# HGRN scan and Hyena gate on one core: a second order table, searched with late loads

## The chip, the cores and the metric

The kernel runs on one core of one Trainium2 chip. The metric is the device time of one execution in microseconds (us), the median over several runs of the same program. A core has TensorE (PE) for matmuls, VectorE (DVE), ScalarE (ACT) and GpSimd (POOL) for the rest, and SyncE (SP), which here only issues the DMAs. Each engine runs its own instructions in order and waits for the others on semaphores.

## The reference, cut to what matters

x and f_logit are 4 x 6272 x 256 in float32. First comes a gated recurrence along the sequence, then a gate with a long convolution (as long as the sequence, circular) between two matrix products:

```python
sig = 1 / (1 + np.exp(-f_logit))
f = lower_bound + (1 - lower_bound) * sig
for t in range(S):                       # S = 6272
    h = f[:, t] * h + (1 - f[:, t]) * x[:, t]
    y[:, t] = h
proj = y @ w_proj                        # 256 -> 3 * 256: x1, x2, x3
X2 = np.fft.rfft(x2, n=S, axis=1)
H = np.fft.rfft(filter_fft, n=S, axis=0)[None]
x2_conv = np.fft.irfft(X2 * H, n=S, axis=1)
out = (x1 * x2_conv * x3) @ w_out
```

## The kernel before, in words

**The stages.** The four batches are worked through one after the other, overlapped at their ends. `hgrn(b)` reads the sequence in 13 chunks (0 to 12) of 512 rows, the last of 128. For each chunk two loads of 512 KB bring f_logit (`FL`) and x (`XT`) into a slot (L318, the DMA is recorded at L331). ScalarE makes the sigmoid in place (`sig`, L334), GpSimd the product with x (`u`, L336). TensorE transposes both halves of the features (`su`, kh = 0 and 1, L348); ScalarE or VectorE turns the gate into f (`f`, L361 or L363), VectorE scans (`scan`, L369), and GpSimd copies the sequence's head behind its end (`wrap`, L292). The result h stays in SBUF (`HA`).

The convolution is a two-stage Fourier transform (6272 = 128 x 49) made of matmuls. `spectrum(b)` runs phase P (x2, L703, copied at L280 or L285), F1 (L716) into the region `A`, F2 (L778), the product with the filter's spectrum (on VectorE straight from PSUM, L801, or a copy on ScalarE and the product on GpSimd, L810), and I2 (L820). The filter's own spectrum is computed at the start and put out to DRAM (L660); `H` loads (L756) bring it back in parts for each batch. `gate(b)` makes x1 * x3 (L397, copies L282 and L287, product L418, or L427 on GpSimd). `phase_o(b)` goes over 13 groups (0 to 12): I1 (L883), the product `y` on VectorE into one of two buffers `ys` (L889), `proj` with w_out (L901), a copy `o` (L282 or L287) into one of six places (two buffers `osb`, two slots of `PP`, two halves of `A`), and the `store` (L913).

**Slots.** x and f_logit have three slots (`NX`), in the first batch three more. The loads of a chunk can be issued when the second transpose step (kh = 1) of the chunk three places before has run. "Chunk 3.11" below is chunk 11 of batch 3 (batches count from 0).

**Who sets the order.** Nothing is scheduled when the kernel is built. Every piece of work is recorded as an op (`Plan.op`, L77) with the engines that may run it, what it reads and writes, and for transfers `dma`, `lag` and `margin`, which `emit` does not read. Then `emit` (L108) runs the ops in the order of the string `ORDER` (L125 to L189): three characters each give the op's number, the engine that runs it and the PSUM bank.

```python
for i, e, b in self.order():
    o = self.ops[i]
    assert e in o["cost"] and i not in seen and o["preds"] <= seen
...
    o["fn"](*args)
```

The table was found by a search outside this file. So the position of a DMA in the string is its place in SP's queue, and SP waits at a load until its slot is free, at a store until its copy is done. An op of one engine that stands behind another op of the same engine can't pass it.

Of the kernel before, what the change touches and what calls it, by code (L numbers as in the profile page):

```python
# [61 lines left out]
class Plan:  # L62
# [63 lines left out]
    "A3gA7gAzgA/gAAYAOYAVIA0YA4AAhQAcQABIACIAPIASYAQAAWIAjQAaQAbQAdQAfQAgQAeQA5QA1SAoUBAYAiUA2KA8ABHgBfgBPgAlUBBUArWAnWBD"  # L126
    "gBLgBXgBTgBbgBjgA9WAsSA6ABIYBJSBCMBEYAyAARAAYUAwVDqgDrgDngAkVD2gECgADgD3gDpgEOgDogEDgEPgEagAqVBQIA+OAXIBFQAmVBRWAuVB"
    "SGApVBGAAZEBKKBYIAUIBMYBNSATYBUYAxVBZWBgABOKBaOAtVBVQBWABcIAvUBhWBiOBdUBkYBeEBlQBmIBpUBqMBwQBxIBnWBoODsAD4ADtYEEAB3U"
    "BuQBvIBrYAEYByYBsWBtOB4EDuSBzQB+UB0AB5WD5YDyQB/EB6GCAUEQACBEDvKDwKB7YEFYCCYB8SDzID0ID6WB9CCDUCEED+QCJSCQUD/AEcAEmgD7"
    "OD8OERYEbgCKKCRMCOWEAIEngEygEGSCHUCIMCPGEHCEIKEoAEdYCLYCSYEKWCTQELGCMUCUACNEEMOESSCZQETKCXWE0AEWUCaICYGCeQCgWEUKE8gE"  # L130
    "zgAFgE9gFGgFQgCGgEpYEJYCbYEXMEYME+ACfAChGCcSCdCEeQEiWEjGEfIEgICnUCoECpSEqUEkOAIACqCCjQCwSCuWErECiYE1YAJYCkAEsMEuQFIA"
    "CvGCsUCxKE2SCzWEvIEwICtEC+UC0GE3KE4KE5QCrYAHYAKYCyYC/EE/YE6ADAWE7IDBGC3UFASC5WFSAC4EDDQC6GFDUDEAC8WC9GEhYFHgFbgF6gFJ"
    "YCVgFRgCmgC7YFTYDCYFagCFgFkgFlgB2gFugCWgDGgFvgAGgFcAFBKFCKFKSDJQJTWJUXFEMFFMFLKDKAJWHJVODOUDPEFmAFMKDHQFNWDIAJYUFOOF"
    "POJaEFUSDQQFVCDRADMUFWKFXWFdYDNEFwAFnYDLYEtYALYDSYAMYEVYElYFxYDXQFYOFZOFeSDYADTUFfCFhQDUEDZWFgKFiADaGFjIFoUFpEDeSDfC"
    "DgWDhGFrQFySDcWFqMJZUJdVFzKF0KF1SFsAMugB1gC2gF4gGlgG3gF/gDWgClgDFgMigMWgF5gC1gMXgD1YEBYExYJXYANYDxYD9YDbYF7YF8YDiYFt"
    "IF2KF3KDdGDjWJbsJeQJiRENAEZAJfFGHSGTUJkBJgoDkOGVQGJWGWIGICMwAGUEGKOGXSGFQGZUGYCGGIGaEMkAGBWGRSGDUGSCGLQGNSGCOMYAGEMG"
    "MIGOKGPUGQEJjWJnXJoQJluJpHJqoGbUDmgDlgHAgMjgDVgGugGdSGhWGcEGeKGfQGmUJsSGiGGgAGosGqsF9WJuCJtTHTgHJQJxSJvrF+GGjUJzCGvW"
    "GkMHKAG4SHLUG8CG6CGrYMZYGxuGzuGnYGwYGpYGsQG5YJyWJ2SJ3TG9YG0YG7YGyYGtAHMEG1QHBUG2AJ0uJ4KJ5rHFsHDsHPWHNQJ7TJ8SKAVHQGG+"
    "WKBUJ9DHOAJ+qHRQHUSKCNHSIG/GHYCMlYHWqKFVKGQKHFKIoKDsHVYHCYHGYHEYHHWHcgMvgGAgHlgHdSHfqHhqHIGHmQH3WHZYKEYHqAHXYHaUHgYH"
    "eYHrYHooHpYHiYHnYH4GHbEKKSKLRKMCKNBH5WHjUH7SH6OHvQHugIBgHkEH8CH9UH+EHsWHzoHxoICSHtGH/UIAMIEqIGCKPRMaWKRBJwYHwYH0YMxY"  # L140
    "JcYHyYKOYIFYILUMbGMeQIPEIHYIDYMcOMfAH1SKQVH2CMgIKStIKgINsITgIcgM6gIvgIlWImGIISIJCIdQIfAIUWIWGIYuIhAMmSMqUIQYIZYIVYIM"
    "YJmYIOYIXYI4gM7gNGgNHgJBgMrEMnKMsMMoKKUWKWGIRQKVXKZWISAKXvIaQIwUI0sIiYIgYIeYM8AM9YI1YMdYIbAKbGInSIpQKaXKeWKfVKcvIysI"
    "oCIqAIrSKjXKgGIsCKlPIjQKkUKhtIkAKmsItSI5WIuKNIAMyQM2UMzAI7uI9GM0INSgJKgKoSKpTKtWKuXNTgKqCKrrKnYIxYKJYJrYNJYJhYIzYM3E"
    "M4MM+QKvGKwHI2SM/ANCWI3CNAIJCUKySKzTNKQJGsNDGJEENegNEOK0CK1rNOUK3SNUANLAJ/YKsYK2YI+YI8YI6YKdYKxYKTYJHYJ6YKYYJFYNVYI/"
# [840 lines left out]
```

## Time and profile before

| | us |
|---|---|
| median of 3 runs | 455.66 (455.5 to 456.23) |
| the profiled execution's own time | 457.66 |
| its span, first to last instruction | 455.5 |
| TensorE busy | 436.8 |
| VectorE busy | 407.9 |
| ScalarE busy | 392.8 |
| GpSimd busy | 307.6 |
| DMA from HBM and to it | 86.12 and 31.98 MB, 259 GB/s over the span |

PE is TensorE's matmuls, PEld its weight loads, which overlap them. "SPq" is SP's queue of DMA issues. In timelines the first two columns are the start and the length of a stretch in us, and the bracket at the end is the idle time of the engine before it with what ended it. In a list of waits the numbers are the total, how often, and the longest. The granted clock of TensorE was 0.998 of full speed.

### The profile page before, as it was taken

How to read it: one execution, taken by the hardware profiler on the slowest of the kernel's cores; microseconds unless marked ns; L12 is line 12 of the kernel's file. 1: busy time of each engine (PE TensorE's matmuls, PEld its weight loads, DVE VectorE, ACT ScalarE, POOL GpSimd, SP SyncE). 2: the span in 40 equal slices, each digit the busy share in tenths (PEclk: the TensorE clock that was granted, in tenths of full speed). 3: DMA queues.
4: the chain of work that ended last, by engine and by line, in shares of the span. 5: the costliest groups of instructions: out<-in, count | busy, mean ns of one | idle time of the engine just before them, and what ended most of it. 6: DMA issues, size and time to landing. Idle time of an engine off the chain costs nothing.

```text
span 455.5 us, 14537 instructions
## 1 busy us (share of the span) xinstructions
PE 436.8 (96%) x6017; PEld 344.1 (76%) x6017; DVE 407.9 (90%) x456; ACT 392.8 (86%) x545; POOL 307.6 (68%) x287
## 2 busy tenths in 40 slices
PE   8999999999999999999999999999999899999994
PEld 6877778667767889767768988776769797776783
DVE  5889998899999986999999987999999859988973
ACT  5789998889999988999988978999999778998354
POOL 4588994289998642889986626999996505657300
PEclk9999999999999999999999999999999999999999
DMA  8999979767797977559956893589586822763167
GB/s 326 406 402 380 373 254 362 275 217 242 273 322 237 333 250 316 173 172 325 357 195 232 308 358 146 179 293 339 192 309 210 349 115 89 219 199 111 47 266 302
DMA packets 42562, 119.04 MB, mean 261 GB/s; under 512 B 4096, under 2 KB 5760, under 8 KB 42496
## 3 DMA queue, kind: packets, MB, share of 16 engines
q1 hardware_dynamic: 42496, 118.11, 72.7%
q8 instruction: 47, 0.77, 0.7%
q14 instruction: 19, 0.16, 0.1%
HBM read 86.12 MB, written 31.98 MB: 259 GB/s over the span
## 4 chain that ended last, share of the span: by engine, by line
PE 58%; DVE 14%; ACT 8%; issue 5%; DMA 5%; POOL 3%; SPq 0%; DVEq 0%; ACTq 0%; POOLq 0%
PE PS L397 14%; PE PS L820 8%; PE PS L703 7%; PE PS L901 7%; DVE HA L369 6%; PE PS L348 6%; PE PS L716 5%; PE PS L778 5%; DMA FL<-in_f_logit_dram 3%; PE PS L883 3%; DVE ys L889 3%; DMA XT<-in_x_dram 2%; DVE fTs L363 2%; PE PS L633 2%; DVE PP L801 2%
## 5 line engine op out<-in xcount | busy, mean ns | idle before, releaser
L336 POOL TENSOR_TENSOR XT<-XT,FL 128x1024 f32<-128x1024 f32 (+1 forms) x47 | 105.1, 2239 | 59.5 <-ACT FL L334 31.7
L369 DVE TENSOR_TENSOR_SCAN HA<-fTs,HA,PS 128x512 f16<-128x512 f32 (+1 forms) x96 | 112.8, 1204 | 3.0 <-ACT fTs L361 2.2
L397 PE MATMUL PS<-HA,W 128*128 128x490 f16 (+1 forms) x416 | 100.4, 367 | 0.3 <-ACT XS L282 0.2
L810 POOL TENSOR_TENSOR PP<-HA,Hu 98x1008 f16<-98x1008 f16 x43 | 90.2, 2106 | 4.3 <-ACT HA L280 2.0
L280 ACT CAST HA<-PS 128x1024 f16<-128x1024 f32 (+1 forms) x106 | 83.5, 821 | 4.9 <-PE PS L716 1.8
L889 DVE TENSOR_TENSOR ys<-PS,zt 128x1024 fp32r<-128x1024 f32 (+1 forms) x52 | 58.5, 1153 | 9.7 <-PE PS L883 5.4
L801 DVE TENSOR_TENSOR PP<-PS,Hu 98x1008 f16<-98x1008 f32 x53 | 62.2, 1199 | 1.5 <-PE PS L820 0.7
L901 PE MATMUL PS<-Wo,ys 128*128 128x256 f32 x392 | 57.8, 293 | 3.3 <-DVE ys L889 2.6
L361 ACT ACTIVATE fTs<-PS,nomc 128x512 f32<-128x512 f32 (+1 forms) x84 | 55.8, 673 | 4.7 <-PE PS L348 2.3
L397 PEld LDWEIGHTS <-W 128*128 128x128 f16 x416 | 35.2, 97 | 29.9 <-issue 3.3
L820 PEld LDWEIGHTS <-PP 98*128 98x128 f16 x1024 | 48.9, 98 | 11.3 <-issue 2.9
L418 DVE TENSOR_TENSOR zt<-PS,XS 128x490 f16<-128x490 f32 (+1 forms) x86 | 54.7, 653 | 2.3 <-DVE XS L287 0.5
L282 ACT ACTIVATE XS<-PS 128x490 f32<-128x490 f32 (+1 forms) x85 | 49.0, 584 | 8.7 <-DVE zt L418 5.1
L901 PEld LDWEIGHTS PS<-Wo,ys 128*128 128x128 f32 x392 | 49.5, 188 | 8.3 <-ACT PP L282 1.5
L280 ACT CAST Th<-PS 128x784 f16<-128x784 f32 x63 | 51.7, 823 | 4.0 <-PE PS L820 3.3
L820 PE MATMUL PS<-VA,PP 98*128 98x98 f16 x512 | 52.0, 207 | 0.8 <-POOL PP L783 0.3
L820 PE MATMUL PS<-VB,PP 98*128 98x98 f16 x512 | 51.8, 207 | 0.0
L334 ACT ACTIVATE FL<-FL 128x1024 f32<-128x1024 f32 (+1 forms) x47 | 47.4, 1012 | 3.0 <-DMA FL<-in_f_logit_dram 2.8
L703 PE MATMUL PS<-W,HA 128*128 128x256 f16 x392 | 43.8, 273 | 0.0
L703 PEld LDWEIGHTS <-HA 128*128 128x128 f16 x392 | 42.8, 142 | 0.7 <-ACT XS L282 0.3
L348 PE MATMUL PS<-iden,FL 64*128 64x64 f32 x704 | 40.3, 230 | 2.7 <-ACT osb L282 1.4
L348 PEld LDWEIGHTS PS<-iden,FL 64*128 64x128 f32 x704 | 30.2, 138 | 15.1 <-DVE HA L369 3.4
(112 smaller groups left out, 764.8 us busy)
## 6 DMA issues: line engine op xcount, KB each, us to landing
FL<-in_f_logit_dram SPq DMA_DIRECT2D x43, 512.0 KB, 5.9
XT<-in_x_dram SPq DMA_DIRECT2D x43, 512.0 KB, 6.7
Hu<-H SPq DMA_DIRECT2D x39, 512.0 KB, 4.4
out_dram<-osb SPq DMA_DIRECT2D x24, 512.0 KB, 4.6
out_dram<-PP SPq DMA_DIRECT2D x16, 512.0 KB, 5.2
Hl<-H SPq DMA_DIRECT2D x13, 512.0 KB, 4.5
out_dram<-HA SPq DMA_DIRECT2D x8, 512.0 KB, 6.1
X<-in_moe_filter_fft_dram SPq DMA_DIRECT2D x7, 512.0 KB, 6.2
```

Of the source, the lines that this page charges most:

```text
L280: nc.scalar.copy(dst, src)
L336: op("u", {"POOL": 0.1 + 0.553 * nb}, lambda e, xt=xt, ft=ft: nc.gpsimd.tensor_tensor(xt, xt, ft, op=AOP.mult), r=[("ft", k)], w=[("xt", k)])
L348: nc.tensor.transpose(bank(pb)[:, at[p] + j:at[p] + hn:nb], src[ps, j, cols], iden[ps, ps])
L361: nc.scalar.activation(fT, sT, AF.Identity, scale=by, bias=1.0)
L369: nc.vector.tensor_tensor_scan(h, fT, bank(pb)[:, 512 - hn:512 + hn], init, op0=AOP.mult, op1=AOP.add),
L397: nc.tensor.matmul(PS[:, p, 0:n], W13[:, kh, js], HA[:, HB[kh] + t0:HB[kh] + t0 + n], start=(kh == 0), stop=(kh == 1))
L703: nc.tensor.matmul(pp[:, r - r0, :], column(HB[kh], q_of(r)), W2[:, kh, :], start=(kh == 0), stop=(kh == 1))
L801: nc.vector.tensor_tensor(pr, px.unsqueeze(1).broadcast_to([TB, 2, UE, 63]), hh(), op=AOP.mult)
L810: nc.gpsimd.tensor_tensor(pr, spec[:, o, :, 1:64].unsqueeze(1).broadcast_to([TB, 2, UE, 63]), hh(), op=AOP.mult)
L820: nc.tensor.matmul(PS[:, ib + o, pr * TB:(pr + 1) * TB], PP[:TB, k, o, n, 2 * pr:2 * pr + 2, :], v[:TB], start=(n == 0), stop=(n == 1))
L889: nc.vector.tensor_tensor(late["ys"][:, yk, :, 0:rn * 128], PS[:, cb:cb + 2, 0:rn * 128], late["zt"][:].rearrange("p k r m -> p k (r m)") ...
L901: nc.tensor.matmul(po[:, i, :], late["ys"][:, yk, kh, i * 128:(i + 1) * 128], Wo[:, kh, :], start=(kh == 0), stop=(kh == 1))
```

## The change

Only the string `ORDER` differs. The new table comes from a search that counted the loads of x and of the logit as landing far later than all other transfers; the ops, their numbers, their sizes and their code are the same, and so are the matmuls. All lines of the string change, since every op's place is in it:

```diff
--- before.py
+++ after.py
@@ -123,69 +123,69 @@
 ORDER = (
-    "A3gA7gAzgA/gAAYAOYAVIA0YA4AAhQAcQABIACIAPIASYAQAAWIAjQAaQAbQAdQAfQAgQAeQA5QA1SAoUBAYAiUA2KA8ABHgBfgBPgAlUBBUArWAnWBD"
...
-    "YElfQlZglmWlnGldCloglgIlhUlpWluQlqOlrSlvIlwQlxIliElegljglsCltglyg"
+    "AzgA3gA/gA7gBHgBDgBXgAAYAOYABIA0AAyYA4AAhQAcQAjQAaQAbQAdQAfQAgQAeQACIA5QA1SA8YAPIASIBAIAoUBBUBCMAiWAlWAQAARABIYA9WAr"
...
+    "PglmQlYGlpWlgKldMlnAlZglogleglhSlqOluUlrQlvMlwUlxMliCljglsAltglyg"
 )
```

Decoded, the two tables differ as follows. On SP (ft is a load of f_logit, xt of x, s a store of the batch that is being put out):

```
batch 0 to 1
before: s0, ft1.11, s1, s3, xt1.11, xt1.12, ft1.12, s2, ft2.0, ft2.1, s6, s5, xt2.2, ft2.2, s4, s8, ...
after:  ft1.11, s1, xt1.11, ft1.12, s2, s0, xt1.12, s5, ft2.0, ft2.1, ft2.2, s3, xt2.0, s8, xt2.2, ...
batch 1 to 2, after: ft2.11, xt2.11, s1, s0, s2, ft2.12, xt2.12, s3, ft3.0, ft3.1, ft3.2, xt3.1, s7, s8, s5, ...
  (before, s5, s3, s6 and s4 come ahead of the loads of batch 3)
batch 2 to 3
before: xt3.10, ft3.10, s0, s1, ft3.11, xt3.11, s4, s2, ft3.12, xt3.12, s7, s6, s3, s5, s8, s9
after:  ft3.10, xt3.10, s1, ft3.11, xt3.11, s3, s0, ft3.12, xt3.12, s2, s9, s4, s8, s6, s5
```

At the start w_out is loaded 25 places earlier and the logit of chunk 0.7 comes behind that of 0.8; some stores and loads of the filter's spectrum change places. On PE the order of steps is nearly the same, with neighbours exchanged: `su` 3.8, kh = 1, now comes ahead of one `proj` and two `I1` of batch 2, and in the last batch `I1` of group 11 comes ahead of `proj` 9, not behind it. Some ops change engine: of the copies of F1, six are on VectorE instead of eight, of those of phase P 28 on ScalarE instead of 31, of the products at L418 84 on VectorE instead of 86; all copies of W are on GpSimd, which also gets the copies of gaps and of the filter's remainder; the masks go from GpSimd to VectorE, and the output copy of group 8 of the last batch to VectorE.

More of the change, by code (lines that the diff above doesn't have):

```diff
@@ L130 @@
[L130 to L144, printed above, removed]
@@ new lines @@
+    "UAnUAsUAwUBJUBEYA6IA+GBPgBLgA2KBQYATYBKMAVYBTgBfgBbgAkWBjgDqgDrgD2gDpgDngD3gDogADgECgEDgAqWAmWBFWBGOBMAEOgAUIEagEPgA"
+    "uUBRUBNSApWAxWBSEBOCBYYBZWAtUBgYBaGBUIBVUBcIBWEAvSBhSBdWAYUBiKBkYAWYBeGDsAAZEBlQBmIBpWBqOBnQBoIBrYBwSBuWBvGBxKBsQB3S"
+    "B5WB4KB6ODtYBtAByYAEYBzQD4AB0ADuSCAWB+UDyQCBGB/EAGgEngEbgEmgEygEzgEEADvKDwKCDUDzID0IB7YD5YAXYCCYEFYB8SCEED6WB9CCHUD7"
+    "OD8OCIECJQD+SCKAEQACQUCRED/KEAKCOWCPGEGQEKUEcAEHIEIICTSCMWELEEMMANYERYCLYCSYEdYEJYCNGCUCESQEWWETIEUIEXGCXUCZSCYECaKE"
+    "oACeUCfEEeQCgSEYOCcUE0AChCFGgCdEEpYCbYCiYEfIEgICnWCjSEiUE1YCpQCkKCoOE8gE9gFIAEjEEkMAFgFHgFQgCGgCWgFbgEqSCqAE+AErCCuQ"
@@ new lines @@
+    "CwWCvIEuUEsKCxGCsQEvEAIYCrYCtACzWE2SDxYE/YCyYEwMC+QC0GE3KE4KE5UDAWE6ME7MC/AC5QFSADBGFASC3WC6AFBCFCKC4GDDQFDUDEAC8WC9"
+    "GFEMF6gFagFRgFFMFkgFJYCFgFlgFugCVgDJSFKQAHYAKYC7YAJYDCYJTWJUXFTYFcAJVGFLIFMIDKCDHUJYWDIMFNSFOKFPKDOQFUUFmAJaGJWHDQWD"
+    "PADMQFVEFWMDRGFdYFnYDLYEhYFXSFwADNADTWFYKFZKDUGFeUFfEDXQFhWFgMDZSDYAFiGDaCFjOFoQDeUB1gDgSFpAC2gB2gDGgFvgC1gF/gG3gClg"
+    "MugDFgCmgFrWMWgMXgDVgF4gDWgGlgMvgF5gEtYDSYALYAMYDfEDhCENYFxYFyUD1YEVYElYEBYDbYExYFqIFzMF0MFsGDjSJZQJdRJXYF7YF8YDiYF1"
+    "UDkCDcSEZAD9AFtOJeWJiXF2MF3MDdCJboMwAJkHJfJGXUGPSJguGQCGHQGYMGFWGIAGGOGZSGTUGRQGSAMYAGUMGaKGVWGBUGNQGWOGCEGOIGDSGEKG"
@@ new lines @@
+    "LUGJQGKAGMMJjWJnXJoSJluGbQJpHJqqGcAGdUGfWGgGGhSGiCGeMGmQJsUF9WJuEGqoGooJtVHJSJxUF+GJvtGjQJzEGvWG4UGkIDmgHAgDlgGAgMig"
+    "GugHKCHLQG8EGzuGxuHTgHcgG0YMZYMxYGwYGnYGpYGrYGsSGyYG9YJyXJ2VHMAHBQGtCG6EMkAJ3WJrYG7YJ4NJ0vJ5uG1UHDoG5YHEYHCYHlgMjgHP"
+    "SJ7WJ8XJ9OJ+vHFoHGYG2EHNUKAQHQCG+SHOEHUWHRUKCAHSMHYGKBQKFRKGXG/CHHUKHBHdSKDoHWuHmQKIvHIEH3UHfqHhqHgYHZYJcYHXYHeYHoAH"
+    "VYHaWHqoHrYHnYHpYHiYKKQKLSH4EHbGH5UKNCKMAHjWH6EH7SHkOHvQH9UH8CH+EHugIBgHsWHzoHxoITgIKgICSH/UIAMIEqMaQKPUHtGIGCMeWILS"
+    "MbAKREMfGMcIIPCKOYMlYHyYH0YHwYJ/YMgOIFYIHYIDYH1UINqIIQKQTKSrH2EIJAIlWIUUIYsImGIWEMmQIdSMnAMqWIhKIfCMoIIZYIMYIQYMrGMs"
@@ new lines @@
+    "OIcgM6gIOYIRUISEKUTKVSIXYJwYKWDKXqIeYJmYIVYIiYIgYIwQIaUM8AM7gIvgKZTI4gKaWKeSNHgNGgJBgIyoI0oIbEInUKbDKfQKgCIoEIpSKjXI"
+    "qCIrUKYYM9YKkRKcuKlPKhoKmpIsEIjSI5WIkCItUI9uI7GIuMMyQM2SMzAM3CKoWKpXKtUKuVM0IKqGKrvNIAKwFM4KM+QNCWM/AKvENAIJCSNDGJGC"
+    "NEONSgNTgKJYJ1YI8YI6YI+YIzYIxYI1YNJYKnYI2UJEqI3EKxYKdYJDYJHYNKQKyTNLANegNfgK0DNUANMIJKgNOWI/UKzSK3TNogNpgNPGK1qNQOJA"
+    "EK5DK4QK6oK8RK9SLBULCTK+BJLWNgAK/qJPuLDELErKTYLFYNVYJ6YNWQLGSNaUNXALICJNGNYINbEKsYMdYLAYKiYJMYJQYK2YK7YJhYNhYJOYKEYJ"
+    "FYJISNiWJJCNcMLHQLLRNlSLMUNjGLJoNkOLNBLOsJRQNqALQVLRWNmCJSANnKLSFRyURzXR0ER1HLKYLTuLPYNNYLUYNrYLaQLVSNygLbINsUNvWNzg"
@@ new lines @@
+    "N8gN9gN0ALWKLcQLXSNwGNxONtENuMLkWLlOLdAOHgOGgN1YLYCLfQN2SN5UN+AN3CN6ELmWLgIN/YNZYM1YLnGLhQLuWN4KN7MLvOOASLiALpQODUOB"
+    "COIALqIOEELwWLrQLxGOQgLegORgOagLjgLZgObgL4WOCKOFMOJYNBYLsAL5OOKSLzUONQOSAL0MOOAOLCL6WL1UOPIL7GL2EOMKL9QNRYMhYOTYMtYO"
+    "cAOdYM5YNFYNdYMpYL+IOUWOVGR3UOXSR4VL/QOYCR5ER6FOWOOZKOeWOhUOfGOgOLygU1gOiEMCSMHWMAAOjMMDKMIOOwUOxEOuQOmSVBgO8WO2UOvA"
+    "VNgLogU2gMBgVOgOnCO9OO0QOyWO1IO3EVDAOzGVPAO4UOqQOoWOrIOpGOsSO6QOkWOtKO5MMESU3AO7AOlGMFCMMUVCgL8gMNMLtgL3gMGgPCWPEQO+"
+    "SPAUPDGPFAMJWMRQPBEO/KPISMKGMSIPGUPoQPHMPQWPMqPKqPSuPpAPNYVEYR8UR9VMOQPLYR2YPTYR7YPJYPRYPUGR+EPOSR/FPYUPVYPcsPasMPAP"
```

82 lines of the change are left out of this document (36 added, 46 removed).

## The prediction

> **What bounds the kernel now.** I read the busy shares first, then the stages, then who waits for whom, then single stretches of the timeline. The shares of the page:
>
> ```profile
> span 455.5 us, 14537 instructions
> PE 436.8 (96%) x6017; PEld 344.1 (76%) x6017; DVE 407.9 (90%) x456; ACT 392.8 (86%) x545; POOL 307.6 (68%) x287
> ```
>
> TensorE is busy 436.8 of 455.5 us. The new table runs the same matmuls, so of the 455.5 us only the 18.7 us in which PE is idle can go; the order can only take from these or add to them. The table by stage shows where they lie (first two columns: length and PE's busy time):
>
> ```profile
> 20.00:50.00 30.00, 28.11 (x345) 22.42 (x344) 28.32 (x33) 28.17 (x38) 23.75 (x25) 1.00 1.01 382
> 50.00:75.00 25.00, 24.80 (x298) 18.91 (x299) 23.67 (x28) 23.85 (x37) 23.27 (x28) 1.00 0.93 330
> 150.00:175.00 25.00, 23.83 (x345) 21.70 (x344) 22.27 (x21) 21.66 (x29) 11.63 (x12) 1.00 0.88 298
> 250.00:275.00 25.00, 24.31 (x350) 22.25 (x350) 22.57 (x21) 20.62 (x28) 10.68 (x9) 1.00 0.92 334
> 350.00:375.00 25.00, 23.07 (x330) 20.90 (x325) 19.29 (x18) 19.71 (x27) 7.67 (x7) 1.00 0.66 255
> 445.00:455.50 10.50, 4.03 (x45) 3.37 (x43) 2.92 (x4) 4.06 (x5) 0.00 (x0) 0.92 0.74 293
> ```
>
> The end has 6.47 us (last copies and stores), 20 to 50 has 1.89, and the three batch boundaries 1.17, 0.69 and 1.93. At a boundary the last chunks of the next batch are scanned while the batch before is multiplied out and stored; there loads and stores share SP. The waits of PE with names (total, times, longest):
>
> ```profile
> PE PS L901 <- DVE ys L889: 2.6, 4, 1.4
> PE PS L348 <- ACT osb L282: 1.4, 1, 1.4
> PE PS L348 <- POOL XT L336: 0.7, 1, 0.7
> PE PS L901 <- ACT X L280: 0.5, 1, 0.5
> ```
>
> These 5.2 us are what a better order has most of. Loads stand behind only part of them, although the waits for loads on other engines look large:
>
> ```profile
> POOL XT L336 <- DMA XT<-in_x_dram: 27.6, 5, 12.6
> SPq L331 <- PE PS L348: 110.0, 40, 10.0
> ```
>
> Most of POOL's 27.6 us is slack, as PE's 0.7 behind it shows. The second row is the rule by which a load is issued: in 40 cases SP waits until the transposes (L348) give the slot back. Sorting the load forward in SP's queue can't bring it ahead of that; it can only remove what stands between release and issue.
>
> **The change part by part.** The ops and their sizes stay; SP's order, some places on the other queues and a few engines change. *Boundary 0 to 1.* SP before (start, duration), then the chain of waits, then VectorE:
>
> ```profile
> 149.49 0.45 SPq L913 DMA_DIRECT2D out_dram<-osb  x1
> 151.52 0.34 SPq L913 DMA_DIRECT2D out_dram<-PP  x1
> 151.96 2.13 SPq L331 DMA_DIRECT2D XT<-in_x_dram  x2
> 154.14 0.48 SPq L331 DMA_DIRECT2D FL<-in_f_logit_dram  x1
> 151.96 7.70 DMA XT<-in_x_dram
> 162.26 0.48 PE PS L348 x8
> 163.48 3.43 DVE L369 TENSOR_TENSOR_SCAN HA<-fTs,HA,PS 128x512 f16<-128x512 f32 x4 [0.57 <-ACT fTs L361]
> ```
>
> The load of x for chunk 11 is issued at 151.96 because a store of PP ahead of it waits for its copy until 151.52. In the new order that store comes after the loads of chunks 11 and 12 and after the next batch's first three logits (2.0 to 2.2). The load then follows the osb store at 149.49 + 0.45 = 149.94, 2.0 us sooner, lands near 157.7, and the 0.70 us wait of PE at 162.26 (row above) has 2 us of room. But VectorE idles only 0.57 us before the scan at 163.48 (last row), and it can't be sooner than its own queue. I take 0.6 us, between 0 and 0.7.
>
> *Boundary 2 to 3.* The logit of chunk 11, behind two rows of the chain for the multiplications and inverse transforms ahead of its release:
>
> ```profile
> 346.82 2.09 PE PS L901 x16
> 348.91 0.56 PE PS L883 x16
> 349.79 7.08 DMA FL<-in_f_logit_dram
> 356.90 1.06 ACT L334 ACTIVATE FL<-FL 128x1024 f32<-128x1024 f32 x1 [1.95 <-DMA FL<-in_f_logit_dram]
> 357.86 1.92 ACT L282 ACTIVATE osb<-PS 128x1024 f32<-128x1024 f32 x2
> 358.92 0.46 PE L348 MATMUL PS<-iden,FL 64*128 64x64 f32 x8 [1.39 <-ACT osb L282]
> 360.45 4.79 DVE L369 TENSOR_TENSOR_SCAN HA<-fTs,HA,PS 128x512 f16<-128x512 f32 x4 [1.35 <-ACT fTs L361]
> ```
>
> ScalarE runs in order: its sigmoid waits 1.95 us for the logit, two output copies (osb) stand behind it, and PE's transposes need the PSUM pair that the first gives back. SP issued this load at its release, so SP's order alone brings nothing. But the new PE order transposes the chunk that gives the slot back (3.8, second half) ahead of one `proj` (8 matmuls: half of 2.09) and two `I1` (16 each: 0.56): 1.05 + 1.12 = some 2.1 us sooner. Then the logit lands near 354.8, ScalarE's 1.95 us close, and PE's 1.39 and VectorE's 1.35 go. Bounds: 1.4 if all of it comes, 0 if the landing slips or the next thing in the queue is late; I take 1.0.
>
> *Boundary 1 to 2.*
>
> ```profile
> 265.47 8.79 DMA FL<-in_f_logit_dram
> 278.20 1.20 PE PS L901 x8
> 279.40 1.80 PE PS L716 x32
> ```
>
> The loads for batch 3 are now ahead of four stores. Only the 0.51 us before 278.20 hangs on this chain, through ScalarE's copies; I take 0, between +0.5 gained and 1.0 lost.
>
> *The end.* After the last inverse transforms PE waits for `ys`, which has two buffers:
>
> ```profile
> 446.09 1.18 PE L901 MATMUL PS<-Wo,ys 128*128 128x256 f32 x8 [0.33 <-DVE ys L889]
> 449.30 1.42 PE L901 MATMUL PS<-Wo,ys 128*128 128x256 f32 x10 [1.36 <-DVE ys L889]
> 447.92 1.56 DVE L889 TENSOR_TENSOR ys<-PS,zt 128x1024 fp32r<-128x1024 f32 x2 [1.98 <-PE PS L883]
> ```
>
> In the new order `I1` of group 11 comes before `proj` of group 9, not after: the multiplication of 1.2 us is then covered by a `proj` of eight matmuls (1.18 us) and more. 1.36 + 0.33 can go; some of it comes back, since VectorE also gets one output copy there, and the end after the last `proj` is as long as before. I take 0.7, between 0 and 1.4.
>
> *The beginning.* One of the copies that move:
>
> ```profile
> L294 POOL TENSOR_SCALAR W<-HA,omc 128x512 f16<-128x512 f32 x2 | 3.2, 1620 | 0.0
> ```
>
> w_out is loaded earlier among the filter's loads, one logit later, and POOL takes a W copy and copies of gaps and of the filter's remainder from ScalarE and DVE, none longer than the 1.62 us of this row. POOL was at 23.75 of 30 and 23.27 of 25 us in the two stages above, so what it gets is hardly hidden there. The chunk products that it makes are due at PE one by one, and a copy in front of one costs at most its length: 1.5 lost is the far end, 0.5 gained the other (the work taken from ScalarE and VectorE comes sooner); I take 0.4 lost.
>
> *Stores behind loads.* This is the new wait. SP runs in order, so a store put behind a load waits for that load's slot. The first store of batch 0, which before left ahead of the row at 149.49, now comes behind the logit of chunk 12 (154.14 in the row above) and another store: some 155.5. Its osb buffer is overwritten by the second of two copies from 159.62:
>
> ```profile
> 159.62 2.15 ACT L282 ACTIVATE osb<-PS 128x1024 f32<-128x1024 f32 x2 [0.34 <-PE PS L901]
> FL<-in_f_logit_dram SPq DMA_DIRECT2D x43, 512.0 KB, 5.9
> XT<-in_x_dram SPq DMA_DIRECT2D x43, 512.0 KB, 6.7
> out_dram<-osb SPq DMA_DIRECT2D x24, 512.0 KB, 4.6
> out_dram<-PP SPq DMA_DIRECT2D x16, 512.0 KB, 5.2
> ```
>
> The second copy starts near 160.7 (half of 2.15 later), so the store has 5.2 us to land. The median of osb is 4.6, and the load of x issued at 151.96 took 7.70: the wait is between 0 and 2.5 us. The Trainium skill (Perfetto Trace Analysis, DMA Instruction — HWDGE) says that the completion can be delayed surprisingly long, above all when the target is HBM. By it the wait would lie nearer its upper end; the medians here don't agree, since stores to HBM landed in 4.6 and 5.2 us, loads of x and the logit in 6.7 and 5.9. I stay with the medians and take 0.4 us for this and its like at the other boundaries.
>
> Sum: -0.6 - 1.0 + 0 - 0.7 + 0.4 + 0.4 = -1.5 us. The profiled execution took 457.66 us with its span of 455.5, 2.0 above the median of 455.66; so 457.66 becomes 456.2, and the median 454.2.
>
> **The rivals.** *All waits go.* The Trainium skill (DMA: Bandwidth & Descriptors, Rules for kernel authors) says to issue a DMA early, do compute, and wait for it late, so that its fixed cost overlaps. If here every load comes early enough, and the tail is covered too, up to 5.2 us of PE's named waits go, against which stand 0.5 of POOL's: 455.66 - 4.7 = 451.0, at most. Against it: release, not queue order, sets most issues (110.0 us, 40 times).
>
> *The loads were hidden, or the gain is swallowed.* DVE has no gap at the boundaries but the ones named, and a place that PE leaves is taken by the next wait on `ys` (2.6 us in four places) or ScalarE; or loads move in the table without being issued sooner, since the slot's release sets them. Then nothing changes beyond what the beginning costs: 455.3, within 0.8 us either way. For it: the issue of 349.79 was at its release. Against it: PE idles where the load was late.
>
> *Stores hold buffers: slower.* If the store of osb lands after 160.7, the copy waits, and behind it in ScalarE's queue stands the fTs copy for which the scan at 163.48 waits. It decides from a landing over 5.2 us; at the 7.70 us of the load beside it, 2.5 us are lost, of which the 0.6 us gained at this place is not to be had either. Two like cases follow: a store of PP and one of the A region of batch 1 now leave behind the loads of batch 3, which took 8.79 us, and the new A and products are written from 279.40 on. One wait of 1 us there and the 2.5 give 455.66 + 3.5 - 1.0 (what boundary 2 to 3 still gains) = 458.2; with only half of it, 456.9.
>
> **How the numbers follow.** Forecast case 0.38, all waits go 0.11, swallowed 0.20, slower 0.31. A measurement of this kernel can tell about 0.2%, 0.9 us. Faster by more: 0.11 of the case where all waits go, and of the forecast case's 0.38 (its own range is 452.9 to 455.2) all but 0.03, so 0.46. Slower by more: 0.31, and 0.05 of the swallowed case's 0.20, so 0.36. The rest, 0.18, is the same. The range goes from 450.9, where all waits go, to 458.8, a little over the full price of held stores; beyond it are the double case and a new stall in a stage that I haven't priced, together under 0.2.
>
> **What would show it.** Right: the load of x for chunk 11 issued near 150, no PE wait on POOL at 162; no wait of ScalarE for the logit near 357, and window 350 to 375 with under 1 us of PE idle; PE's waits for `ys` down by over 1 us after 445. Wrong: ScalarE or SP waits on a store (out_dram) at a boundary, POOL waits that reach PE before 75 us, or PE idle of over 18.7 us in all.

## The result: slower by 0.25%

| | before | after |
|---|---|---|
| median, 20 runs each, us | 456.26 (455.04 to 458.08) | 457.61 (456.39 to 459.06) |
| ratio, 95% interval | | 1.0025 (1.0015 to 1.0036) |
| profiled execution, us | 457.66 | 457.61 |
| its span, us | 455.5 | 455.8 |

By the ratio the new table costs 1.1 us (0.7 to 1.6; the two medians are 1.35 apart), where a gain of 1.5 us was forecast. Two things in this table matter for the rest. The old kernel's runs spread over 3 us. And the profiled execution of before, on which the whole prediction rests, took 457.66 us, 1.4 above the median of its 20 runs, while that of after lies on its median.

The profile after, busy shares and stages (the columns as before):

```profile
PE 437.1 (96%) x6017; PEld 345.2 (76%) x6017; DVE 409.6 (90%) x455; ACT 392.6 (86%) x543; POOL 310.7 (68%) x291
20.00:50.00 30.00, 27.36 (x329) 21.93 (x328) 26.76 (x31) 26.82 (x37) 24.98 (x29) 1.00 1.00 381
50.00:75.00 25.00, 24.96 (x310) 18.80 (x309) 24.37 (x28) 24.37 (x37) 24.73 (x30) 1.00 0.96 347
150.00:175.00 25.00, 24.68 (x367) 22.34 (x364) 22.56 (x21) 22.25 (x30) 13.41 (x14) 1.00 0.82 284
175.00:200.00 25.00, 24.05 (x336) 19.80 (x335) 20.60 (x21) 22.62 (x30) 16.89 (x15) 1.00 0.67 244
250.00:275.00 25.00, 23.83 (x355) 21.57 (x352) 22.85 (x22) 21.46 (x29) 11.15 (x10) 1.00 0.86 301
350.00:375.00 25.00, 24.41 (x339) 22.18 (x338) 20.67 (x20) 20.77 (x27) 11.53 (x11) 1.00 0.59 224
```

TensorE's idle time fell where the forecast said: 150 to 175 from 1.17 to 0.32 us, 350 to 375 from 1.93 to 0.59. It rose elsewhere: 20 to 50 from 1.89 to 2.64, 175 to 200 from 0.14 to 0.95, 250 to 275 from 0.69 to 1.17. In all it is 18.7 us again. A window holds the same times, though, and not the same work: at 250 us TensorE is 2.0 us further back in the new kernel. The table at the end of the experiments compares by matmul, and there the stretch around 275 us is a gain. TensorE's waits:

```profile
PE PS L901 <- DVE ys L889: 1.8, 2, 1.2
PE PS L901 <- ACT HA L280: 0.8, 1, 0.8
PE PS L778 <- DVE HA L369: 0.7, 2, 0.5
PE PS L397 <- DVE PP L801: 0.4, 1, 0.4
```

The waits of L348 on XT (0.7) and on osb (1.4) are gone from the list. New are one of L901 on the A region (HA) and two of F2 (L778) on VectorE's scan, which come up again below. Behind the first stands a store. Chain of waits, then SP's queue, ScalarE and TensorE of the new kernel:

```profile
172.18 9.79 DMA out_dram<-HA
172.18 0.60 SPq L913 DMA_DIRECT2D out_dram<-HA  x1
182.05 2.84 ACT L280 CAST HA<-PS 128x1024 f16<-128x1024 f32 x3 [1.09 <-DMA out_dram<-HA]
183.11 1.10 PE L901 MATMUL PS<-Wo,ys 128*128 128x256 f32 x7 [0.85 <-ACT HA L280]
```

Store 4 of batch 0 now leaves at 172.18, behind six loads of batch 2 and four stores (its copy had been done 13 us before that), and takes 9.79 us. F1 of batch 1 can't write the A region until then: ScalarE waits 1.09 us, TensorE 0.85. In the old kernel it left at 167.40 and had landed at 175.0.

### The profile page after: what moved, and what is told of

The parts are those of the page before. It is cut to its first block, busy times and chain, and to the rows that moved or that the text cites. A ratio compares the mean times of both kernels' runs of the same rounds, so it can differ in the third digit from the quotient of the medians.

```text
span 455.8 us, 14523 instructions
## 1 busy us (share of the span) xinstructions
PE 437.1 (96%) x6017; PEld 345.2 (76%) x6017; DVE 409.6 (90%) x455; ACT 392.6 (86%) x543; POOL 310.7 (68%) x291
## 4 chain that ended last, share of the span: by engine, by line
PE 62%; DVE 16%; DMA 9%; issue 5%; ACT 4%; POOL 3%; SPq 1%; DVEq 0%; POOLq 0%; ACTq 0%
PE PS L397 15%; DVE HA L369 8%; PE PS L703 8%; PE PS L820 7%; PE PS L348 7%; PE PS L901 7%; PE PS L778 5%; PE PS L716 5%; PE PS L883 4%; DVE ys L889 3%; PE PS L633 3%; DMA HA<-in_moe_filter_fft_dram 3%; DMA out_dram<-HA 2%; POOL PP L810 2%; DMA Hu<-H 2%
## 5 line engine op out<-in xcount | busy, mean ns | idle before, releaser
L810 POOL TENSOR_TENSOR PP<-HA,Hu 98x1008 f16<-98x1008 f16 x42 | 88.1, 2105 | 8.5 <-ACT HA L280 3.6
L280 ACT CAST HA<-PS 128x1024 f16<-128x1024 f32 (+1 forms) x107 | 84.8, 831 | 5.0 <-DMA out_dram<-HA 1.1
L801 DVE TENSOR_TENSOR PP<-PS,Hu 98x1008 f16<-98x1008 f32 x54 | 63.6, 1198 | 3.5 <-PE PS L778 0.9
L901 PE MATMUL PS<-Wo,ys 128*128 128x256 f32 x392 | 58.1, 293 | 2.9 <-DVE ys L889 1.8
L361 ACT ACTIVATE fTs<-PS,nomc 128x512 f32<-128x512 f32 (+1 forms) x83 | 54.4, 668 | 4.3 <-PE PS L348 1.6
L820 PEld LDWEIGHTS <-PP 98*128 98x128 f16 x1024 | 49.0, 98 | 10.7 <-issue 2.7
L901 PEld LDWEIGHTS PS<-Wo,ys 128*128 128x128 f32 x392 | 49.5, 188 | 8.3 <-ACT PP L282 2.1
L418 DVE TENSOR_TENSOR zt<-PS,XS 128x490 f16<-128x490 f32 (+1 forms) x84 | 53.6, 651 | 1.8 <-PE PS L397 0.4
L703 PE MATMUL PS<-W,HA 128*128 128x256 f16 x392 | 43.6, 273 | 0.0
L703 PEld LDWEIGHTS <-HA 128*128 128x128 f16 x392 | 42.8, 142 | 0.6 <-issue 0.2
L348 PE MATMUL PS<-iden,FL 64*128 64x64 f32 x704 | 40.2, 230 | 1.2 <-DVE HA L369 0.5
L348 PEld LDWEIGHTS PS<-iden,FL 64*128 64x128 f32 x704 | 30.3, 138 | 13.2 <-issue 3.8
```

Source lines behind the costliest of these rows:

```text
L280: nc.scalar.copy(dst, src)
L348: nc.tensor.transpose(bank(pb)[:, at[p] + j:at[p] + hn:nb], src[ps, j, cols], iden[ps, ps])
L361: nc.scalar.activation(fT, sT, AF.Identity, scale=by, bias=1.0)
L703: nc.tensor.matmul(pp[:, r - r0, :], column(HB[kh], q_of(r)), W2[:, kh, :], start=(kh == 0), stop=(kh == 1))
L801: nc.vector.tensor_tensor(pr, px.unsqueeze(1).broadcast_to([TB, 2, UE, 63]), hh(), op=AOP.mult)
L810: nc.gpsimd.tensor_tensor(pr, spec[:, o, :, 1:64].unsqueeze(1).broadcast_to([TB, 2, UE, 63]), hh(), op=AOP.mult)
```

## The experiments

Both tables run the same ops, so they can be joined: the old table up to a place where both have run the same ops, the new one behind it, or the other way round. In the diffs below `old[a:b]` is a piece of the string by op count, and a sum leaves out ops that have run already. The times that are named are the old kernel's.

**First, the new table up to each batch's phase P.**

```diff
-ORDER = old
+ORDER = new[:phase P of batch b] + old      # cut0, cut1, cut2, cut3: b = 0, 1, 2, 3
```

> The new table up to the first step of phase P of batch 0 (about 72 us), the old table behind it. Theory (the forecast gains came at the boundaries and were outweighed by new waits elsewhere): the beginning alone costs what the two traces show there, the same matmul 0.6 us later at 77 us, so +0.4 to +1.0 us against before. Rival 1 (the beginning is the whole loss): +1.2 us or more, and the same in the three longer cuts. Rival 2 (the loss is in the last batch and the tail): 0.

> The new table up to the first step of phase P of batch 1 (about 167 us; the boundary 0 to 1 with its loads is in it, the late stores behind it are not), the old table behind it. Theory: the beginning +0.6, batch 0's transform stage (100 to 122 us) +0.8, boundary 0 to 1 -0.7, so +0.5 to +1.0 us. Rival 1: +1.2 or more, as the shortest cut. Rival 2: 0.

> The new table up to the first step of phase P of batch 2 (about 265 us), the old table behind it. Theory: the shorter cut plus the wait of ScalarE for a store of the A region at 182 us (+1.1), so +1.5 to +2.1 us: the largest loss of the four. Rival 1: +1.2, as the shortest cut. Rival 2: 0.

> The new table up to the first step of phase P of batch 3 (about 366 us), the old table behind it (with two pairs of PSUM banks exchanged by name). Theory: batch 2's stage and boundary 2 to 3 gain 2.1 us against the cut before, so -0.4 to +0.3 us. Rival 1: +1.2 as the shortest cut. Rival 2 (all loss in the last batch and tail): 0 or below, and then all four cuts are at 0 or below.

| run | median, us | before, measured beside it | ratio (95%) |
|---|---|---|---|
| cut0 | 459.25 | 456.31 | 1.0068 (1.0048 to 1.0088) |
| cut1 | 459.55 | 456.31 | 1.0074 (1.0056 to 1.0092) |
| cut2 | 458.57 | 456.31 | 1.0047 (1.0029 to 1.0064) |
| cut3 | 457.99 | 456.31 | 1.0034 (1.0020 to 1.0047) |

No theory had 2.9 us at the first cut. The trace shows that the joint makes most of it:

```profile
PE PS L703 <- ACT X L280: 3.0, 1, 3.0
```

The new table issues the logit of 1.1 later, and the old part's sigmoid for it, early in ScalarE's queue, holds the copies of phase P until it has landed. cut1 has a like wait (L703 on ys, 2.1 us). So the two say little of the tables. cut2 and cut3 have none of that size. cut2 is as slow as expected, 2.1 us; cut3 is a miss, 1.6 us slower where 0.3 was to be the most. What the four traces do show, side by side, is the old order's spread. In the stretch of boundary 2 to 3, where cut0, cut1 and cut2 run the old order, the same matmuls came 1.2, 1.4 and 0.4 us sooner than in the first profile.

**Second, joints at clean places, the end alone, and the late store.**

```diff
+ORDER = old[:145 us] + new                  # rev145
+ORDER = new[:145 us] + old                  # cut145
+ORDER = old[:430 us] + new                  # revtail
 new table, SP                               # a_store
-s5, ft2.0, ft2.1, ft2.2, s3, xt2.0, s8, xt2.2, xt2.1, s7, s4, s6
+s5, s4, ft2.0, ft2.1, ft2.2, s3, xt2.0, s8, xt2.2, xt2.1, s7, s6
```

> The old table up to 145 us (where both tables have run the same ops, but for one small copy on GpSimd), the new table behind it. Theory 2 (the waits at boundaries 0 to 1 and 2 to 3 that the forecast wanted to remove, 0.7 and 1.4 us, were accidents of the one profiled execution, which took 457.66 us, so there was little to gain there; the new table loses about 1.5 us before 145 us and 1 us at a late store, and gains some 1 us in batch 2's transform): 1.4 us below the new table, so 0 to -0.5 us against before. Rival (the boundary waits are regular in the old table and the gain of 2.1 us is real, the beginning loses 2.9): -1.3 us or more. Trace of both: no ScalarE wait for the logit near 356 us.

> The new table up to 145 us, the old one behind it. Theory 2: +1.3 to +1.7 us against before, and the old order's waits at boundaries 0 to 1 (0.7 us) and 2 to 3 (1.4 us) absent or smaller in this look although the old order runs there. Rival: +2.5 to +3 us, and both waits there as in the profile before.

> The old table up to 430 us (same ops run in both), the new table for the last 60 ops alone. The forecast had this part at -0.7 us. The trace of the new table says 0: the last wait of TensorE for ys is 1.25 us there, against 1.36, since the product of group 11 writes the ys buffer that proj of group 9 still reads. Theory 2: -0.2 to +0.4 us. Rival (the forecast's step is right, the trace was an accident): -0.7 us.

> The new table with one DMA moved: the store of group 4 of batch 0 (from the A region) goes to SP right behind the store of group 5, ahead of the logits of 2.0 to 2.2, as its copy is done by then. Theory 2 and the forecast's slower rival: the wait of ScalarE for out_dram<-HA at 182 us (1.09 us, 0.85 on TensorE) is gone, and the time is 0.7 to 1.1 us below the new table's, so +0.2 to +0.6 us against before. Rival (VectorE or another wait takes the place): as the new table, +1.3.

| run | median, us | before | ratio (95%) |
|---|---|---|---|
| rev145 | 457.75 | 456.43 | 1.0030 (1.0015 to 1.0045) |
| cut145 | 458.34 | 456.43 | 1.0041 (1.0029 to 1.0053) |
| revtail | 458.92 | 456.43 | 1.0057 (1.0044 to 1.0070) |
| a_store | 457.13 | 456.43 | 1.0018 (1.0009 to 1.0027) |

rev145 and cut145 are both slower, by 1.3 and 1.9 us; in both traces TensorE loses near 1 us at the joint (135 to 147 us), and revtail has the end's PSUM banks exchanged, with 4.1 us of waits for ys instead of 2.6. These three were misses. a_store moves one store and nothing else. Its ScalarE, where after had the 1.09:

```profile
180.08 1.05 ACT L282 ACTIVATE PP<-PS 128x1024 f32<-128x1024 f32 x1
181.09 2.84 ACT L280 CAST HA<-PS 128x1024 f16<-128x1024 f32 x3
```

The wait is gone. The ratio of 1.0018 stands against 1.0025: about 0.3 us less, where 0.7 to 1.1 was expected, with intervals that overlap. So the trace shows what the late store holds up, and the times don't tell its price from nothing. In cut2, where the store also leaves late (172.3) but landed in 8.6 us, at 180.8, there was no wait either; in cut3 and rev145 it took 10.6 and 10.7 us, and the wait was there. So the rival is right in kind: by the traces it costs TensorE about 1 us in the executions in which it strikes, three of four.

**Third, the forecast's own steps, each alone.**

```diff
 old table, SP                               # b_sp01
-s1, s3, xt1.11, xt1.12, ft1.12, s2
+s1, xt1.11, xt1.12, ft1.12, s3, s2
 old table, TensorE, last batch              # b_tail
-proj 10, proj 9, I1 11, I1 12, proj 11, proj 12
+proj 10, I1 11, proj 9, I1 12, proj 11, proj 12
+ORDER = old[:82 us] + new[:180 us] + old    # mid, with a_store's store
+ORDER = old[:287 us] + new                  # rev287
```

> The old table with one store moved: at boundary 0 to 1 the PP store of group 3 goes behind the loads of chunk 11 (x) and 12, so that the load of x for chunk 1.11 leaves some 2 us sooner; nothing else differs. This is the forecast's step for that boundary done alone. The forecast: -0.6 us, from a wait of 0.70 us of TensorE that goes. Theory 2 (the wait was an accident of the profiled execution: three other executions of the old order there had 0.4 us or less of TensorE idle before phase P in place of 1.04): 0, within 0.3 us, though the load is issued 2 us sooner.

> The old table with I1 of group 11 of the last batch ahead of proj of group 9, as in the new table, with PSUM banks to suit; nothing else differs. This is the forecast's step for the end done alone. The forecast: -0.7 us. Theory 2 (the product of group 11 can't start before proj of group 9 has read the same ys buffer, so the wait of 1.36 us before proj of group 11 stays): the wait 1.2 to 1.4 us, the time within 0.3 us of before.

> The old table up to 82 us, the new one from there to 180 us (with the store of the A region moved forward as in the run a_store), then the old one again. It isolates batch 0's transform stage, where all traces of the new order lose 0.8 us between 109 and 122 us, and boundary 0 to 1. Theory 2: +0.6 to +1.0 us against before. Rival (the stage's loss is made up before 180 us, and the loss of the new table is the beginning's): 0 or below.

> The old table up to 287 us, where both tables have run exactly the same ops, and the new one behind it. It holds the parts of the new table that gained in the traces (batch 2's transform -0.7, boundary 2 to 3 -0.4 against the old order's mean over its executions) without those that lost (the beginning, batch 0's transform, the late store at 182 us). Theory 2: -0.7 to -1.3 us against before, faster than both kernels. Rival (no part gains): 0 or above.

| run | median, us | before | ratio (95%) |
|---|---|---|---|
| b_sp01 | 455.78 | 456.44 | 0.9990 (0.9978 to 1.0001) |
| b_tail | 456.46 | 456.44 | 1.0005 (0.9993 to 1.0016) |
| mid | 456.52 | 456.44 | 1.0005 (0.9992 to 1.0018) |
| rev287 | 463.14 | 456.44 | 1.0153 (1.0137 to 1.0169) |

b_sp01 lies between the two expectations, and its interval just takes in 1: the step is worth somewhere from nothing to 1 us. mid is a miss: level with before (+0.2 us by the ratio, from -0.4 to +0.8), where +0.6 to +1.0 was expected. b_tail brings nothing. Its end, TensorE and VectorE:

```profile
444.41 1.21 PE L901 MATMUL PS<-Wo,ys 128*128 128x256 f32 x8
446.00 0.29 PE L883 MATMUL PS<-ID,Th 64*128 64x128 f16 x4 [0.39 <-ACT PP L282]
446.99 1.45 PE L901 MATMUL PS<-Wo,ys 128*128 128x256 f32 x10 [0.70 <-DVE ys L889]
445.71 1.55 DVE L889 TENSOR_TENSOR ys<-PS,zt 128x1024 fp32r<-128x1024 f32 x2 [1.60 <-PE PS L901]
```

VectorE waits for L901, not for I1 (L883) as before: the product of group 11 writes the `ys` buffer that `proj` 9 (444.41) still reads. The wait for ys fell from 1.36 to 0.70 rather than staying, but a wait for a PSUM bank (0.39) came with it. Counted from 432 us the last matmul starts 0.44 us sooner, and the span ends 5.4 us behind its start, not 5.0. rev287 was spoilt by its joint: a product that the old table gives to GpSimd stands at an empty place of the new one, behind a step that waits, and TensorE lost 7 us there.

**Fourth, the beginning, and the later part again.**

```diff
+ORDER = old[:287 us] + new                  # rev287b: pm of unit 0 ahead of the gate's product
+ORDER = old[:180 us] + new                  # rev180
+ORDER = new[:82 us] + old                   # beg82: sigmoid of 1.1 moved back
+ORDER = new[:180 us] + old                  # cut180: with a_store's store
```

> The old table up to 287 us and the new one behind it, as in the run rev287, but with one product of GpSimd (pm of unit 0 of batch 2) put ahead of the gate's product. In rev287 that step stood where the new table, in which it is done on VectorE, has an empty place for it, and TensorE lost 7 us there between 280 and 301 us. Theory 2: -0.7 to -1.3 us against before. Rival (the later part gains nothing): 0.

> The old table up to 180 us, where both tables have run the same ops, the new one behind it. Without the beginning, batch 0's transform and the late store. Theory 2, by the traces (192 to 288 us +0.2, 288 to 353 us -0.7, boundary 2 to 3 -0.4, behind it 0): -0.6 to -1.2 us. Rival: 0.

> The new table up to 82 us, the old one behind it, with the sigmoid of chunk 1.1 moved back on ScalarE to where its product follows (otherwise ScalarE waits there for a load that the new table issues later, which cost 3 us in cut0). Theory 2: the beginning costs +0.3 us by the traces, so 0 to +0.6. Rival 1 of the first call (the beginning is the whole loss): +1.2 us or more.

> The new table up to 180 us, with the store of the A region moved forward as in a_store, the old table behind it. Theory 2: the beginning +0.3 and batch 0's transform +0.8: +0.8 to +1.4 us. Rival (the transform's loss is made up at boundary 0 to 1): +0.3 or less, as beg82.

| run | median, us | before | ratio (95%) |
|---|---|---|---|
| rev287b | 457.59 | 456.44 | 1.0022 (1.0009 to 1.0035) |
| rev180 | 456.30 | 456.44 | 1.0002 (0.9989 to 1.0014) |
| beg82 | 461.85 | 456.44 | 1.0120 (1.0102 to 1.0139) |
| cut180 | 456.43 | 456.44 | 1.0002 (0.9991 to 1.0012) |

beg82 (a wait of I2 for GpSimd, 3.7 us) and rev287b (1.5 us of F1 on a scan, just ahead of the joint) pay again for the joining: neither whole table has these waits at anything like that size. rev180 and cut180, both joined at the place where the sets of ops agree, are level with before, and both miss what theory 2 expected: the later part of the new table gains nothing that these times show (from 0.5 us gained to 0.6 lost), and its first 180 us, with the store moved forward, cost nothing (from 0.4 gained to 0.5 lost).

**Fifth, the old kernel itself again, and the best of both.**

```diff
+ORDER = old                                 # same
+ORDER = old[:180 us] + new[:378 us] + old   # best, with b_sp01's store
```

> The old kernel itself, unchanged. Both theories: ratio 1 within 0.1%. What is looked for is its trace: theory 2 expects that the waits of the first profile at boundaries 0 to 1 (0.70 us) and 2 to 3 (1.39 us) are smaller or absent, and last differences to that profile of 1 to 2 us at the last matmul; the forecast took them as regular.

> The old table, with the PP store of boundary 0 to 1 moved behind the loads (as in b_sp01) and with the new table's order from 180 to 378 us. By the traces' sections (median of the looks, new against old): 191 to 272 us -0.1, 272 to 288 +0.3, 288 to 354 -0.7, and b_sp01's -0.2 to -0.6. Theory 2: -0.5 to -1.0 us, faster than both kernels, if only by about the bound of what a measurement can tell. Rival (gains of single sections don't add up, since a stretch that is ahead waits at the next): 0.

| run | median, us | before | ratio (95%) |
|---|---|---|---|
| same | 456.05 | 456.28 | 0.9999 (0.9988 to 1.0010) |
| best | 455.99 | 456.28 | 0.9993 (0.9983 to 1.0002) |

best isn't told apart from before. The trace of same is the one that settles the forecast. Same code, second profile: TensorE at boundary 0 to 1, then ScalarE and TensorE at boundary 2 to 3:

```profile
161.94 0.63 PE L883 MATMUL PS<-ID,Th 64*128 64x128 f16 x16
162.38 0.43 PE L348 MATMUL PS<-iden,FL 64*128 64x64 f32 x8
162.75 0.46 PE L348 MATMUL PS<-iden,XT 64*128 64x64 f32 x8
356.34 1.06 ACT L334 ACTIVATE FL<-FL 128x1024 f32<-128x1024 f32 x1 [0.72 <-DMA FL<-in_f_logit_dram]
358.37 0.46 PE L348 MATMUL PS<-iden,FL 64*128 64x64 f32 x8 [0.16 <-ACT osb L282]
```

The wait of 0.70 us isn't there, and that of 1.39 us is 0.16. The load of x took 6.9 us and the logit 5.9, against 7.7 and 7.1 in the first profile. Elsewhere this execution lost 0.9 us, between 95 and 135 us, where the first lost nothing; its own time, 457.11 us, is 0.8 above the median of 456.28 without the two waits.

**All traces together.** The start of the same matmul, counted from the first, was compared in all 20 traces with the first profile. A negative number says that TensorE did that stretch faster than there. The stretches begin and end at matmuls ahead of which all kernels have run the same matmuls, so that neighbours exchanged between the tables don't count. Left out are a run's stretches with a joint in them or upset by one close by, and those in which its own step lies (b_sp01 and best from 158 to 178, b_tail in the last row). Medians in us:

```
stretch, us     old order (traces)   new order (traces)   new - old
  1 to  71      +0.07 (11)           +0.63 (8)            +0.6
 71 to  95      +0.02 (10)           -0.10 (7)            -0.1
 95 to 134      -0.01 (11)           +0.81 (8)            +0.8
134 to 158       0.00 (11)           +0.18 (7)            +0.2
158 to 178      -0.69 (10)           -0.72 (7)             0.0
178 to 191       0.00 (11)           +1.05 (4, late store) +1.1
191 to 263      -0.01 (13)            0.00 (7)             0.0
263 to 286      -0.20 (11)           -0.62 (6)            -0.4
286 to 354      -0.01 (12)           -0.08 (6)            -0.1
354 to 366      -1.37 (12)           -1.43 (7)            -0.1
366 to 432       0.00 (11)           +0.28 (6)            +0.3
432 to 450       0.00 (12)           -0.20 (6)            -0.2
```

The rows 158 to 178 and 354 to 366 are the two boundaries of the forecast. There the old order is as fast as the new, in the median; the 0.7 and 1.4 us are what the first profile lost and most others didn't. (In the row 354 to 366 the old order's twelve run from 0 to -1.5, the new order's from -0.6 to -1.45; in 158 to 178 one more old trace, rev180, has the wait: 0.9 us, with the load of x at 7.9 us.) The sections in the expectations above were counted by the matmul's number alone, which is other work where neighbours are exchanged. That is why they have a loss from 272 to 288 and a gain of 0.7 from 288 to 354; counted as here, it is a gain of 0.4 and then hardly any.

## Why the prediction was wrong

**The step that failed: sizing a gain from one execution.** The prediction read two waits, 0.70 and 1.39 us, as what the old order costs. It saw that the profiled execution lay 2.0 us above the median then shown, and took the same 1.5 us off both, when the difference was as large as those waits: 0.7 + 1.4 = 2.1. (Against the median of all 20 runs it is 1.4.) In the nine other traces that run the old order unchanged at boundary 0 to 1, the load of x for 1.11 landed in 6.6 to 7.9 us, and TensorE waited in one of them; at boundary 2 to 3 the logit of 3.11 landed in 4.4 to 6.7 us in the eleven others, and TensorE's wait was nothing in seven of them, 0.1 or 0.2 in two, 0.65 and 1.0 in the other two. The mean landing of a load after batch 0 in the first profile was 6.07 us, the longest of the 20 traces (the others 5.53 to 5.98).

**Boundary 0 to 1** (-0.6 forecast). The mechanism holds: x of 1.11 left without the PP store ahead of it, and no wait was left in the new trace. SP's queue of the new kernel:

```profile
151.05 0.38 SPq L913 DMA_DIRECT2D out_dram<-osb  x1
151.52 0.38 SPq L331 DMA_DIRECT2D XT<-in_x_dram  x1
```

By the clock that is only 0.4 us sooner than 151.96, and not the "near 150" that the prediction named as its sign, since TensorE came to this place 1.6 us later; counted from the second transpose step of chunk 1.10, the load is 2.0 us sooner, as forecast. The size is nil in the median; b_sp01, the step alone, came out 0.5 us faster by the ratio, with an interval from 1.0 us down to nothing.

**Boundary 2 to 3** (-1.0). The mechanism holds here too. New kernel:

```profile
354.85 1.27 ACT L361 ACTIVATE fTs<-PS,nomc 128x512 f32<-128x512 f32 x2
356.00 1.06 ACT L334 ACTIVATE FL<-FL 128x1024 f32<-128x1024 f32 x1
358.50 0.41 PE L348 MATMUL PS<-iden,FL 64*128 64x64 f32 x8
```

The logit was issued 2.1 us sooner, counted from I1 of group 9 beside it, as forecast. It landed at 353.9, the sigmoid waited for nothing, the transposes neither. In the median it brought 0.1 us, with less spread.

**Boundary 1 to 2** (0, bounds +1.0 lost and 0.5 gained): from 263 to 286 us the new order gains 0.4 in the median. The wait of 0.5 us of L901 for ScalarE's copy ahead of 278.20 is in none of its six traces, and the old order's eleven run from -0.57 to +0.55 there. The term was inside its bounds, near the gaining end.

**The end** (-0.7). Wrong in its mechanism. The prediction looked at what covers the product and not at which of the two `ys` buffers it writes. New kernel:

```profile
449.07 1.41 PE L901 MATMUL PS<-Wo,ys 128*128 128x256 f32 x10 [1.25 <-DVE ys L889]
447.69 1.56 DVE L889 TENSOR_TENSOR ys<-PS,zt 128x1024 fp32r<-128x1024 f32 x2 [0.48 <-PE PS L901]
451.06 0.42 DVE L287 TENSOR_SCALAR osb<-PS 128x256 f32<-128x256 f32 x1 [1.81 <-DMA out_dram<-osb]
```

The wait stays at 1.25, and the last copy now waits for a store of osb. From the start of the last matmul to the end of the span it is 5.6 us in the new order's traces (median) against 5.0 in the old's, so the prediction's "the end after the last `proj` is as long as before" failed too. The wait of the last copy is not the cause: the last store is issued 1.6 us behind the last matmul in all 20 traces. It takes longer to land (the kernel before, then after, stores issued from 447 us on):

```profile
out_dram<-osb SPq DMA_DIRECT2D x1, 128.0 KB, 2.6
out_dram<-osb SPq DMA_DIRECT2D x1, 128.0 KB, 3.1
```

It lands behind the store of group 11, and that one in all 20 traces 1.2 to 1.3 us behind the store of group 9, which the earlier matmul does not hurry: in b_tail the last matmul starts 0.44 us sooner, and 0.35 of it is lost again at the end.

**The beginning** (+0.4, bounds -0.5 and +1.5): +0.4 in the traces (up to 95 us). The size held, and that was luck in part: the term was priced by copies that GpSimd gets, but most of the waits of TensorE before 75 us that only the new trace has are for ScalarE and VectorE (0.2 to 0.3 us each); the one for GpSimd grew from 0.2 to 0.4 there.

**Stores behind loads** (+0.4, bounds 0 and 2.5). The mechanism of the slower rival, and the prediction's own sign of being wrong ("ScalarE or SP waits on a store"), at another place than priced: store 4 of batch 0 and the A region at 182 us, not store 0 and osb at 160.7. About 1 us where it strikes. The median landings of the new kernel:

```profile
FL<-in_f_logit_dram SPq DMA_DIRECT2D x43, 512.0 KB, 5.3
XT<-in_x_dram SPq DMA_DIRECT2D x43, 512.0 KB, 6.6
out_dram<-osb SPq DMA_DIRECT2D x24, 512.0 KB, 5.4
out_dram<-HA SPq DMA_DIRECT2D x8, 512.0 KB, 5.4
```

By the Trainium skill (Perfetto Trace Analysis, DMA Instruction — HWDGE) the completion of a DMA can be delayed surprisingly long, above all when it writes to HBM. The medians still don't bear that out as a rule, 5.4 us for these stores against 5.3 and 6.6 for the loads; the one store that decided took 9.79. By the medians the prediction took 0.4 us for the wait, the single landing made it 1.1.

**A term that was missing.** Batch 0's transform (95 to 135 us) was not priced at all, since the diff does not point to loads there; seven of the eight traces of the new order lose 0.8 us in it, mid 0.3. VectorE of the new kernel, where a gap lies, and then TensorE, whose F2 (L778) waits twice for VectorE's scan:

```profile
114.80 1.21 DVE L801 TENSOR_TENSOR PP<-PS,Hu 98x1008 f16<-98x1008 f32 x1 [0.46 <-ACT HA L280]
117.84 0.61 PE L778 MATMUL PS<-HA,FT 64*128 64x256 f16 x8 [0.20 <-DVE HA L369]
129.22 0.61 PE L778 MATMUL PS<-HA,FT 64*128 64x256 f16 x8 [0.47 <-DVE HA L369]
```

In the old trace VectorE has no gap of that size between 108 and 122 us. The two waits of F2, 0.7 us together, are in all eight traces of the new order and in none of the eleven of the old. The engines changed there too: 134 of the 2419 ops run on another engine than before, far more than the net counts in the section on the change let one see. This is read from the traces; no run changed that stretch alone without a joint.

**A slip that changed little.** In the rival where the loads were hidden, the beginning's cost of 0.4 us was taken off: 455.66 + 0.4 is 456.1, not 455.3.

**What stays open.** With 0.55 us at the end the medians of the stretches add up to 2.5 us, and 1.1 (0.7 to 1.6) were measured; the old kernel's executions each lose something somewhere (same: 0.9 at 95 us; b_sp01: 1.2 before 71 us), which medians by stretch leave out. cut180 should by the table be 1.4 us slower (the first five rows), and was level, within 0.5. Nor do the parts add up: rev180 and cut180 together hold the whole new table with the store moved forward, and cost 0.2 us by their ratios, while a_store, which is that table, cost 0.8 (0.4 to 1.2). So it is shown that the forecast's gains were accidents of one execution, and what the late store holds up; how much of the rest the first 180 us hold, waits of F2 included, isn't settled. Nor do the runs show a table better than the old one by more than the spread: b_sp01 and best are 0.1% below it, with intervals that take in 1.

## What to carry to other kernels

Before a wait in a profile is priced as a gain, compare the profiled execution's own time with the median of the runs: where it is above by as much as the waits at hand, these may be what sets it apart, and a second profile of the same code can tell. A load given more slack frees what stood behind it only in the executions in which it was late; what was moved back for it (here a store that holds a region) can be late in more of them, here in three of four. When a product is to be covered, look up which buffer it writes and who still reads that. And when two orders are compared by the start of a matmul, take one ahead of which both have run the same work.

## What the runs showed of the hardware

One program's transfers do not land alike from one execution to the next: the logit of chunk 3.11 took 4.4 to 7.1 us under the old order's issue, one store of 512 KB 8.6 to 10.7 us at nearly the same place in the queue, and where they were late TensorE was up to 1.4 us later. By contrast, three stretches of the old order, 134 to 158, 178 to 191 and 366 to 432 us, came out alike within 0.02 us in eleven traces each. The Trainium skill (DMA: Bandwidth & Descriptors, Rules for kernel authors) advises to issue early and wait late. The new table does so with its loads, and at the two boundaries of the forecast it gains 0.1 us at most in the median, since the loads it helps held TensorE up in few executions.
